# Softmax weights of the first 24 steps normalised by the product that turns them

## The chip, the core and the metric

The kernel runs on one core of a Trainium2 chip. The metric is the device time of one execution in microseconds (us). The engines are PE (TensorE), DVE (VectorE), ACT (ScalarE), POOL (GpSimd) and SP (SyncE, which only starts transfers). Each of them takes its instructions in the order in which they stand.

## What is computed

A windowed attention for 4 batches of 8 heads, 768 positions and 64 channels. Each query sees the first 8 keys and the 96 keys up to its own, with a bias that grows with the distance. Behind it stands a gated projection over 512 channels.

```python
scores = scale * (q @ k.T) + bias                  # 0.125, -slope[h] * distance
scores = where(keep, scores, -1e9)                 # keep: key < 8, or 0 <= query - key < 96
a = exp(scores - max(scores))
a = a / (sum(a) + 1e-9)
x = a @ v                                          # heads side by side: 512 channels
gate = sigmoid(sum_k conv_w[k] * shifted(x, k))    # 5 taps along the sequence
out = (gate * (x @ w_val)) @ w_out
```

## The kernel before

**Groups and steps.** The attention is cut into 32 groups g of one batch, one half of the sequence (384 queries) and one pair of heads. Four groups in a row make a phase: one batch and half, all 8 heads; there are 8 phases. A group has three steps s of 128 queries, 96 in all. A step holds its scores for the two heads j in 168 columns each (96 + 8 + 64); the very first step of each sequence has 128.

**The kinds of operation**, by the names that the tables use:

- S g (L624): PE multiplies queries and keys of a group into two PSUM banks, one for each head, as products of 64 rows by 64 columns.
- AM s,j (L632): DVE adds the bias, scales, and keeps the row's minimum. S of the next group waits for the AM of this one.
- EX s,j (L643): ACT takes the exponential into the tile `p` and adds up each row's sum in `sm`.
- RG, RC (L650, L654): the sums of a batch of steps are guarded and inverted into `rs`. The first three steps are batches by themselves, after that a batch has three steps in a first half and two in a second half of the sequence.
- NM s,j (L660, L662): `p` is multiplied row by row with the reciprocal sum, on POOL, DVE or ACT.
- PT (L675): PE turns `p` of a whole batch, 64 query rows at a time, into the two banks `pt`. It is a transposition by the identity, with 104 or 128 columns of `p` loaded as weights and 64 columns streamed: four of them for a step of 128 columns and six for any other.
- EV (L297, L299): ACT or DVE copies the two banks into `ab`, and PT of the next batch waits for that.
- PV (L702, L709): PE multiplies values and turned weights of two groups into `x`.
- XS, XH, XL, CV, SG: `x` is copied out, split into a high and a low part for PE, and filtered by five taps into `gate`.
- VM (L836): PE multiplies phase, output block m and input block c, three products of 384 columns each. GM, GH, GL (L843 on) gate the result and split it.
- OM, OE, ST (L859, L871): PE projects to the output in products of 512 columns; the result is copied out and stored.
- W..., WS (L539 to L541): the weights come as 64-bit numbers and are taken apart; WS is PE's part of that, for the first four blocks.
- WARM and F (L406): products of constants into a bank that nobody reads. WARM stands at the program's start; the three F have 4, 7 and 6 products.

**What sets the order.** Nothing is scheduled at run time. `SLOTS` is a table with a place for every operation, `ENGINES` a table with the engine of those that may run on more than one; the program is written out in the order of the places. `plan.ring` adds the waits of a set of buffers: with `P_B = 7` tiles `p`, for example, EX of a step waits for the PT that frees the tile used seven steps ahead.

Of the kernel before, what the change touches and what calls it, by code (L numbers as in the profile page):

```python
# [16 lines left out]
WARM, FILL_N = 10, (4, 7, 6)  # L17
# [3 lines left out]
HEAD_STEPS, RS_B = 3, 3  # L21
W_PARTS = (2, 2, 2, 2, 2, 1, 1, 1)
# [3 lines left out]
        1, 4, 6, 17, 93, 122, 124, 168, 173, 251, 294, 298, 353, 405, 437, 444, 604, 608, 615, 619, 650, 705, 822,  # L26
        917, 921, 983, 1008, 1012, 1060, 1221, 1227, 1358,
    ),
    "LB": (3,),
    "LV": (  # L30
        18, 97, 129, 134, 177, 182, 209, 213, 240, 247, 349, 409, 428, 432, 497, 501, 710, 713, 724, 727, 813, 816,
        914, 991, 1002, 1064, 1211, 1215, 1224, 1353, 1356, 1496,
    ),
    "WARM": (2,),
    "F": (22, 86, 50),
    "IOTA": (0,),
    "UNITS": (15,),
    "CNT": (7,),
    "DIST": (9, 13),
    "BIAS": (16, 21, 12, 24, 39, 20, 11, 19),  # L40
# [10 lines left out]
    "CWL": (10,),  # L51
    "CWA": (113,),
    "CW": (117,),
    "S": (
        14, 37, 67, 106, 142, 180, 217, 254, 311, 347, 394, 434, 473, 504, 535, 591, 642, 696, 726, 787, 817, 894,
        919, 978, 1041, 1087, 1117, 1170, 1220, 1292, 1363, 1447,
    ),
# [1115 lines left out]
```

## Time and profile before

| | us |
|---|---|
| median of 3 runs | 258.26 (257.35 to 259.97) |
| the profiled execution | 257.78 |
| its span, first to last instruction | 255.7 |
| PE busy | 246.2 (96%) |
| DVE busy | 225.1 (88%) |
| ACT busy | 188.5 (74%) |
| POOL busy | 141.0 (55%) |

The profile is of one execution, and its time is 2.1 us over its span. Shares of busy time are means over stages with different limits, and a matmul's record lasts longer than the time until the next one may start, so PE's busy time is read through the distance between starts.

### The profile page before, as it was taken

To read this page: it belongs to the slowest core of one execution; us is meant where nothing else is said; L and a number is where in the kernel's file an instruction comes from. 1 tells how busy PE (TensorE), PEld (TensorE's weight loads), DVE (VectorE), ACT (ScalarE), POOL (GpSimd) and SP (SyncE) were. 2 spreads that over 40 slices of the span, in tenths; PEclk is the share of its full clock that TensorE was granted. 3 is DMA by queue.
4 is the path that set the end of the run, shared out by engine and by line. 5 is a ranking of instruction groups with operands and counts; after the bars stand their busy time and mean duration, and the time that the engine had idled before them with its cause. 6 is when DMAs were issued, how large, how long until landed. Compare 5 with 4: busy or idle time off the path is not lost.

```text
span 255.7 us, 8994 instructions
## 1 busy us (share of the span) xinstructions
PE 246.2 (96%) x3384; PEld 207.5 (81%) x3386; DVE 225.1 (88%) x783; ACT 188.5 (74%) x643; POOL 141.0 (55%) x240
## 2 busy tenths in 40 slices
PE   8878899999999999999999999999999999999993
PEld 3546678887879987898888998899889889888983
DVE  4999999999999999999999899988999896169940
ACT  3899999999989998888795999685457545055410
POOL 5697999999786687426435554435405602631210
PEclk9999999999999999999999999999999999999998
DMA  5859996367315661532337600650160041010203
GB/s 152 319 179 326 380 359 222 126 219 255 124 45 171 240 235 45 163 119 66 134 122 266 208 3 4 207 225 3 56 224 0 3 154 73 0 44 3 82 5 127
DMA packets 16302, 36.36 MB, mean 142 GB/s; under 512 B 1920, under 2 KB 4480, under 8 KB 16256
## 3 DMA queue, kind: packets, MB, share of 16 engines
q1 hardware_dynamic: 16112, 35.75, 40.2%
q8 instruction: 28, 0.46, 0.7%
q14 instruction: 18, 0.15, 0.2%
q10 hardware_dynamic: 144, 0.00, 0.0%
HBM read 29.46 MB, written 6.29 MB: 140 GB/s over the span
## 4 chain that ended last, share of the span: by engine, by line
PE 50%; DVE 33%; ACT 6%; POOL 6%; issue 3%; DVEq 0%; POOLq 0%
PE o L859 17%; PE val L836 16%; DVE gate L794 11%; DVE t L632 8%; PE s L624 5%; PE pt L675 4%; POOL p L662 4%; PE x L709 3%; ACT p L643 3%; DVE p L662 2%; PE warm L406 2%; PE x L702 2%; DVE g L843 2%; DVE ab L299 2%; DVE xl L786 1%
## 5 line engine op out<-in xcount | busy, mean ns | idle before, releaser
L643 ACT ACTIVATE p<-t,mins 128x168 f32<-128x168 f32 (+1 forms) x192 | 81.0, 427 | 10.3 <-PE pt L675 4.8
L794 DVE SCALAR_TENSOR_TENSOR gate<-xs,cwt,gate 128x384 f32<-128x384 f32 x128 | 81.8, 657 | 1.2 <-ACT gate L796 0.4
L662 POOL TENSOR_SCALAR p<-p,rs 128x168 f32<-128x168 f32 (+1 forms) x100 | 54.9, 559 | 18.3 <-DVE rs L654 13.2
L632 DVE CUSTOM_DVE_ANT_0 t<-s,bias 128x168 f32<-128x168 f32 (+1 forms) x192 | 53.8, 316 | 2.4 <-PE s L624 2.4
L836 PE MATMUL val<-xh,wvh 128*128 128x384 f32 x128 | 44.8, 350 | 0.1
L836 PE MATMUL val<-xl,wvh 128*128 128x384 f32 x128 | 43.3, 338 | 0.1
L836 PE MATMUL val<-xh,wvl 128*128 128x384 f32 x128 | 43.2, 338 | 0.0
L859 PE MATMUL o<-woh,gh 128*128 128x512 f32 (+1 forms) x100 | 39.9, 399 | 0.0
L859 PE MATMUL o<-wol,gh 128*128 128x512 f32 (+1 forms) x100 | 38.6, 386 | 0.0
L859 PE MATMUL o<-woh,gl 128*128 128x512 f32 (+1 forms) x100 | 38.6, 386 | 0.0
L624 PE MATMUL s<-kq 64*64 64x64 f32 (+3 forms) x1088 | 36.6, 264 | 1.7 <-DVE mins L632 0.9
L650 POOL TENSOR_SCALAR sm<-sm 128x4 f32<-128x4 f32 (+2 forms) x32 | 11.0, 344 | 49.1 <-ACT p L643 47.3
L624 PEld LDWEIGHTS s<-kq 64*64 64x64 f32 x1088 | 31.4, 133 | 8.2 <-issue 4.2
L643 ACT ACTIVATION_READ_ACCUMULATOR p<-t,mins 128x1 f32 x192 | 37.3, 194 | 0.0
L297 ACT COPY ab<-pt 128x384 f32<-128x384 f32 (+3 forms) x60 | 29.1, 494 | 9.6 <-PE pt L675 9.3
L850 POOL TENSOR_TENSOR gl<-g,gh 128x384 fp32r<-128x384 f32 x21 | 23.1, 1104 | 19.7 <-ACT gh L297 7.6
L675 PEld LDWEIGHTS pt<-ident,p 64*104 64x104 f32 (+1 forms) x544 | 19.2, 131 | 10.2 <-issue 5.1
L675 PE MATMUL pt<-ident,p 64*104 64x64 f32 (+1 forms) x544 | 25.0, 226 | 1.2 <-DVE cw_h L596 1.1
L836 PEld LDWEIGHTS val<-xh,wvh 128*128 128x128 f32 x128 | 24.0, 188 | 2.2 <-DVE ob L873 0.4
L660 ACT ACTIVATE p<-p,rs 128x168 f32<-128x168 f32 (+1 forms) x55 | 22.5, 426 | 4.2 <-DVE rs L654 4.2
L836 PEld LDWEIGHTS val<-xl,wvh 128*128 128x128 f32 x128 | 24.1, 188 | 0.9 <-DVE xl L786 0.5
L709 PE MATMUL x<-ab,va 104*64 104x128 f32 (+1 forms) x384 | 24.7, 277 | 0.0
(157 smaller groups left out, 414.4 us busy)
## 6 DMA issues: line engine op xcount, KB each, us to landing
kq<-in_kq SPq DMA_DIRECT2D x16, 444.0 KB, 5.7
va<-in_va SPq DMA_DIRECT2D x16, 384.0 KB, 4.3
out<-ob SPq DMA_DIRECT2D x24, 256.0 KB, 2.6
kq<-in_kq SPq DMA_DIRECT2D x15, 392.0 KB, 5.5
va<-in_va SPq DMA_DIRECT2D x16, 320.0 KB, 4.8
w<-in_wv SPq DMA_DIRECT2D x8, 256.0 KB, 5.4
w<-in_wo SPq DMA_DIRECT2D x3, 512.0 KB, 3.5
w<-in_wo SPq DMA_DIRECT2D x2, 256.0 KB, 5.6
```

What stands on the lines that cost most here:

```text
L297: nc.scalar.copy(dst, src)
L624: nc.tensor.matmul(s[rows, u : u + w], T["rq", g][r, k * P + half * QH : k * P + (half + 1) * QH], T["rk", g][r, c : c + w], start=True, s ...
L632: nc.vector.tensor_tensor_reduce(out=t[:, :n], in0=T["s", s // HB, s % HB, j][:, :n], in1=bias[:, h, :P] if n == P else bias[:, h, P:], op ...
L643: nc.scalar.activation(T["p", s][:, j, :n], T["t", s, j][:, :n], AF.Exp, bias=mins[:, s, j : j + 1], scale=-1.0, accum_out=T["sm", batch_o ...
L660: nc.scalar.mul(pr, pr, rs)
L662: engine(e).tensor_scalar(out=pr, in0=pr, scalar1=rs, scalar2=1.0, op0=ALU.mult, op1=ALU.mult)
L675: nc.tensor.transpose(pts[h][:m, c0 : c0 + QH], pr[rows, c : c + m], ident[rows, rows])
L709: nc.tensor.matmul(T["x", g][rows(i), c0 : c0 + P], T["near", g][:n, k, j], T["a", HB * g + k][:n, j * P : (j + 1) * P], start=False, stop ...
L794: nc.vector.scalar_tensor_tensor(out=gt, in0=src, scalar=w, in1=gt, op0=ALU.mult, op1=ALU.add)
L836: nc.tensor.matmul(T["val", ph, m], (wvh, wvh, wvl)[r][:, m, c * P : (c + 1) * P], (T["xh", g], T["xl", g], T["xh", g])[r], start=(c == 0 ...
L850: engine(e).tensor_sub(tile_of(("gl", ph, m), [P, HT], F32R, "gl", 5), T["g", ph, m], T["gh", ph, m])
L859: nc.tensor.matmul(T[key][:, cols], (T["gh", ph, c], T["gl", ph, c], T["gh", ph, c])[r][:, rows], (woh, woh, wol)[r][:, c, cols], start=(c ...
```

## The change

In the first 24 steps (12 batches) there is no NM. Instead a new operation DG on DVE or POOL builds, for each batch, one 64 by 64 diagonal of reciprocal sums for every step and head and each half of the rows, in one instruction: the identity folded to 128 rows of 64 columns (FOLD, once) times `rs`. PT then multiplies `p` with this diagonal where it multiplied with the identity. These are products, not transpositions, and each block of 104 or 128 columns is cut in two, since its columns belong to two heads or must land at partition 0 and at 64. There is one buffer for the diagonals (`DG_B = 1`), so a DG waits for the PT of the batch ahead. F keeps its first four products; thirteen are gone. Places and engines of all operations are new.

```diff
-WARM, FILL_N = 10, (4, 7, 6)
+WARM, FILL_N = 10, (4,)
+DIAG_STEPS, DG_B = 24, 1
...
-        "VVGVGGGGGGGSVGGSGSGVSGGSGGGGGGGSGGGVGSGGGGVGGGGSSGSGSGSGGVSGGGGVSGGGGGGGVSSVGVGGVSGGSGSSGVVGGGSG"
+        "SGSGGGGGGSVSSSGSGGSGSGSSGSSGVSVSVGGSSGSGSSGSVSGSSSSVSGSSSGSVGSSGGGVGGSVSVSGGVVGSVGGGSSSGGSSSVGGG"
...
+    "DG": (41, 51, 95, 102, 135, 164, 195, 239, 258, 278, 307, 321),
...
+    "DG": "GVVGVVVVGVVG",
...
+    def fold_ident(e):
+        T["fold",] = const.tile([P, QH], F32, name="fold")
+        engine(e).tensor_add(T["fold",], ident[:, :QH], ident[:, QH:])
...
+    def diag(e, ss):
+
+        n = 2 * len(ss)
+        t = tile_of(("dg", ss[0]), [P, 2 * HB, QH], F32, "dg", DG_B)
+        engine(e).tensor_tensor(out=t[:, :n], in0=T["fold",].unsqueeze(1).to_broadcast([P, n, QH]),
+                                in1=T["rs", ss[0]][:, :n].unsqueeze(2).to_broadcast([P, n, QH]), op=ALU.mult)
+
+    def turn(ss):
+
+        c0 = 0
+        for s in ss:
+            pr = T["p", s].rearrange("p two n -> p (two n)")
+            n = width(s)
+            m = P if n == P else SH
+            near = [[(c, 0, QH, j), (c + QH, QH, m - QH, j)] for j, c in ((0, 0), (1, SW if n == P else 2 * SW - SH))]
+            for block in near + ([] if n == P else [[(SH, 0, QH, 0), (SW, QH, QH, 1)]]):
+                for h in range(2):
+                    rows = slice(h * QH, (h + 1) * QH)
+                    for c, r, w, j in block:
+                        nc.tensor.matmul(pts[h][r : r + w, c0 : c0 + QH], pr[rows, c : c + w],
+                                         T["dg", ss[0]][rows, 2 * (s - ss[0]) + j], start=True, stop=True)
                 c0 += QH
...
-                         [("RG", ss[0])] + plan.ring("rs", RS_B, key, [("NM", t, j) for t in ss for j in range(2)]))
-            for j in range(2):
+                         [("RG", ss[0])] + plan.ring("rs", RS_B, key, [("DG", ss[0])] if ss[0] < DIAG_STEPS else
+                                                     [("NM", t, j) for t in ss for j in range(2)]))
+            folded = ss[0] < DIAG_STEPS
+            if folded and s == ss[-1]:
+                key = ("DG", ss[0])
+                plan.add(key, (DVE, POOL), lambda e, ss=ss: diag(e, ss),
+                         [("RC", ss[0]), ("FOLD",)] + plan.ring("dg", DG_B, key, [("PT", ss[0])]))
+            for j in () if folded else range(2):
                 plan.add(("NM", s, j), (POOL, DVE, ACT), lambda e, s=s, j=j: norm(e, s, j), [("RC", batch_of[s])])
...
-                plan.add(key, (PE,), lambda e, ss=ss: transpose(ss),
-                         [("NM", t, j) for t in ss for j in range(2)] + [("IOTA",)] + bank)
+                plan.add(key, (PE,), lambda e, ss=ss, turned=turn if folded else transpose: turned(ss),
+                         ([("DG", ss[0])] if folded else [("NM", t, j) for t in ss for j in range(2)] + [("IOTA",)])
+                         + bank)
```

What this moves is seen at three places. On PE, the first two PT stood around the second F (`p_184` and `p_195` are the weights of steps 0 and 1, the `s` that follows is group 2's):

```order
L675 MATMUL pt_89<-ident,p_184 128x64
L675 MATMUL pt_90<-ident,p_184 128x64
...
L406 LDWEIGHTS const-bfloat16-1.0
L406 MATMUL warm<-const-bfloat16-1.0 128x512
...
L675 MATMUL pt_89<-ident,p_195 104x64
L675 MATMUL pt_90<-ident,p_195 104x64
...
L675 MATMUL pt_89<-ident,p_195 128x64
L675 MATMUL pt_90<-ident,p_195 128x64
L624 MATMUL s_0_283<-kq_131 64x128
```

and now follow each other as products of 64 by 64 and 40 by 64:

```order
L706 MATMUL pt_89<-dg_229,p_187 64x64 x2
L706 MATMUL pt_90<-dg_229,p_187 64x64 x2
...
L706 MATMUL pt_89<-dg_254,p_198 64x64
L706 MATMUL pt_89<-dg_254,p_198 40x64
L706 MATMUL pt_90<-dg_254,p_198 64x64
L706 MATMUL pt_90<-dg_254,p_198 40x64
...
L706 MATMUL pt_89<-dg_254,p_198 64x64 x2
L706 MATMUL pt_90<-dg_254,p_198 64x64 x2
L633 MATMUL s_0_289<-kq_135 64x128
```

The F between them is gone, and every product of PT has the 64 by 64 shape of the S that follows. On POOL, the batch of steps 3 to 5 (`rs_340`) had five of its six NM behind each other:

```order
L650 TENSOR_SCALAR sm_256<-sm_256 128x6
L662 TENSOR_SCALAR p_228<-p_228,rs_306 128x168
L498 TENSOR_SCALAR ('w', 1)_z<-w_135 128x512
L662 TENSOR_SCALAR p_270<-p_270,rs_340 128x168
L662 TENSOR_SCALAR p_280<-p_280,rs_340 128x168
L662 TENSOR_SCALAR p_255<-p_255,rs_340 128x128
L662 TENSOR_SCALAR p_270<-p_270,rs_340 128x168
L662 TENSOR_SCALAR p_255<-p_255,rs_340 128x128
L650 TENSOR_SCALAR sm_321<-sm_321 128x6
```

and has one DG in their place (`rs_392`):

```order
L507 TENSOR_SCALAR ('w', 1)_z<-w_139 128x512
L502 TENSOR_SCALAR ('w', 1)_y<-w_139 128x512
L659 TENSOR_SCALAR sm_252<-sm_252 128x6
L691 TENSOR_TENSOR dg_398<-fold,rs_392 128x384
L659 TENSOR_SCALAR sm_330<-sm_330 128x6
L507 TENSOR_SCALAR ('w', 2)_z<-w_322 128x512
```

What filled POOL between two guards is one instruction now, and preparation of the weights moves up. On PE again, from the S of group 6 (`s_0_688`, now `s_0_739`) to that of group 7 (`s_0_807`, now `s_0_870`) there stood PV, PT, the first VM (`val_0`), and only behind S the WS of weight block 3:

```order
L624 MATMUL s_0_688<-kq_440 64x168
...
L702 MATMUL x_718<-ab_614,va_450 64x64 x2
...
L675 MATMUL pt_89<-ident,p_548 104x64
...
L836 MATMUL val_0_792<-xh_625,wvh 128x384
...
L624 MATMUL s_0_807<-kq_573 64x168
...
L539 MATMUL pt_90<-('w', 3)_h,ident 128x512
```

and now the first VM and one more (`val_1`) stand ahead of both S, and that WS between them:

```order
L875 MATMUL val_0_697<-xh_635,wvh 128x384
...
L875 MATMUL val_1_711<-xh_635,wvh 128x384
...
L633 MATMUL s_0_739<-kq_459 64x168
...
L706 MATMUL pt_89<-dg_732,p_548 64x64
...
L734 MATMUL x_799<-ab_609,va_607 64x64 x2
...
L548 MATMUL pt_90<-('w', 3)_h,ident 128x512
...
L633 MATMUL s_0_870<-kq_637 64x168
```

So PE has one WS and one VM more behind it when it comes to group 7's S.

## Rows read from the trace of the kernel before

**Rows 1.** The page: span, busy time and instructions, and slices of 6.4 us

```profile
span 255.7 us, 8994 instructions
PE 246.2 (96%) x3384; PEld 207.5 (81%) x3386; DVE 225.1 (88%) x783; ACT 188.5 (74%) x643; POOL 141.0 (55%) x240
...
DVE  4999999999999999999999899988999896169940
...
PEclk9999999999999999999999999999999999999998
```

**Rows 2.** Windows of 16 us: busy us of each engine (instructions), clock, DMA

```profile
16.00:32.00 16.00, 13.05 (x292) 9.83 (x294) 15.31 (x65) 15.28 (x59) 13.68 (x24) 1.00 0.98 336
32.00:48.00 16.00, 15.89 (x287) 13.36 (x287) 15.69 (x62) 15.83 (x58) 15.47 (x24) 1.00 0.66 240
...
144.00:160.00 16.00, 16.00 (x315) 14.18 (x311) 14.53 (x57) 15.03 (x53) 9.15 (x17) 1.00 0.05 19
```

**Rows 3.** PE's timeline, 8 to 36 us: start, length, [idle ahead <-releaser]

```profile
8.15 1.31 PE L624 MATMUL s<-kq 64*64 64x128 f32 x32 [0.61 <-DVE mins L632]
...
12.80 1.12 PE L539 MATMUL pt<-('w', 0)_h,ident 128*128 128x512 f32 x2
...
14.27 1.70 PE L406 MATMUL warm<-const-bfloat16-1.0 128*128 128x512 bf16 x6
15.90 0.38 PE L675 MATMUL pt<-ident,p 64*104 64x64 f32 x6
...
18.33 0.69 PE L675 MATMUL pt<-ident,p 64*128 64x64 f32 x16 [1.09 <-DVE cw_h L596]
...
19.70 1.13 PE L539 MATMUL pt<-('w', 1)_h,ident 128*128 128x512 f32 x2 [0.68 <-ACT ab L297]
...
25.86 1.11 PE L624 MATMUL s<-kq 64*64 64x168 f32 x34 [0.30 <-DVE mins L632]
...
28.48 1.12 PE L539 MATMUL pt<-('w', 2)_h,ident 128*128 128x512 f32 x2 [0.62 <-ACT ab L297]
...
34.58 1.11 PE L624 MATMUL s<-kq 64*64 64x168 f32 x36
```

**Rows 4.** POOL's timeline, 13 to 18.4 us

```profile
15.04 3.24 POOL L662 TENSOR_SCALAR p<-p,rs 128x168 f32<-128x168 f32 x5
```

**Rows 5.** The chain that ended last, 140 to 236 us: start, length

```profile
143.39 0.49 PE pt L675 x12
143.88 0.95 PE s L624 x27
144.83 0.70 PE x L702 x47
...
164.16 0.72 PE val L836 x3
...
165.57 0.53 PE val L836 x3
...
172.81 0.62 PE pt L675 x16
...
174.47 0.47 PE x L702 x32
...
229.10 0.84 PE x L702 x24
```

**Rows 6.** Groups by line: busy us, mean ns, idle ahead

```profile
L662 POOL TENSOR_SCALAR p<-p,rs 128x168 f32<-128x168 f32 (+1 forms) x100 | 54.9, 559 | 18.3 <-DVE rs L654 13.2 <-ACT ob L871 3.4 <-PE val L836 0.4
...
L660 ACT ACTIVATE p<-p,rs 128x168 f32<-128x168 f32 (+1 forms) x55 | 22.5, 426 | 4.2 <-DVE rs L654 4.2
...
L786 POOL TENSOR_TENSOR xl<-xs,xh 128x384 fp32r<-128x384 f32 x16 | 17.4, 1089 | 8.7 <-ACT xh L297 8.5
...
L662 DVE TENSOR_SCALAR p<-p,rs 128x168 f32<-128x168 f32 (+1 forms) x37 | 13.5, 374 | 0.1
...
L786 DVE TENSOR_TENSOR xl<-xs,xh 128x384 fp32r<-128x384 f32 x16 | 10.1, 634 | 0.0
```

More of the change, by code (lines that the diff above doesn't have):

```diff
@@ L33 @@
     ),
     "WARM": (2,),
[L35 to L40, printed above, removed]
[10 rows of a table removed]
-    "CWL": (10,),
-    "CWA": (113,),
-    "CW": (117,),
+    "F": (21,),
+    "IOTA": (3,),
+    "UNITS": (18,),
+    "FOLD": (35,),
+    "CNT": (8,),
+    "DIST": (10, 13),
+    "BIAS": (14, 19, 16, 24, 36, 40, 17, 20),
[10 rows of a table added]
+    "CWL": (15,),
+    "CWA": (98,),
+    "CW": (120,),
     "S": (
-        14, 37, 67, 106, 142, 180, 217, 254, 311, 347, 394, 434, 473, 504, 535, 591, 642, 696, 726, 787, 817, 894,
-        919, 978, 1041, 1087, 1117, 1170, 1220, 1292, 1363, 1447,
+        11, 38, 65, 91, 122, 159, 200, 238, 275, 305, 342, 396, 446, 488, 512, 551, 595, 658, 725, 781, 808, 865,
+        892, 949, 1006, 1059, 1124, 1176, 1226, 1266, 1337, 1421,
@@ L105 @@
+        1517,
+    ),
+    "DG": (41, 51, 95, 102, 135, 164, 195, 239, 258, 278, 307, 321),
     "PT": (
[L106 to L108 removed]
+        46, 59, 97, 114, 146, 170, 206, 245, 269, 288, 312, 335, 389, 418, 469, 508, 556, 590, 613, 652, 675, 732,
+        777, 801, 863, 886, 945, 970, 1011, 1057, 1076, 1129, 1173, 1192, 1262, 1334, 1353, 1401, 1419, 1433, 1536,
+        1551,
@@ L109 @@
     ),
     "EV": (
[5 rows of a table removed]
-    ),
-    "WS": (78, 127, 202, 261),
-    "ZH": (35,),
[5 rows of a table added]
+    ),
[10 rows of a table added]
+    ),
+    "ZH": (0,),
     "XS": (
-        171, 188, 253, 249, 387, 374, 476, 469, 570, 578, 643, 670, 781, 731, 846, 860, 942, 926, 1004, 1010, 1125,
-        1129, 1188, 1202, 1310, 1355, 1389, 1397, 1568, 1578, 1591, 1599,
+        147, 150, 228, 262, 340, 386, 436, 421, 490, 542, 637, 619, 704, 712, 802, 834, 897, 924, 1005, 1048, 1102,
+        1081, 1193, 1199, 1287, 1307, 1359, 1414, 1434, 1435, 1559, 1565,
@@ L184 @@
-    "FA": (1577,),
-    "FB": (1650,),
-    "FC": (1652,),
+        630, 564, 618, 720, 731, 965, 946, 962, 1135, 1128, 1131, 1179, 1302, 1318, 1340, 1463, 1469, 1487, 1585,
+        1555, 1583, 1622, 1630, 1637,
+    ),
+    "FA": (1508,),
+    "FB": (1613,),
+    "FC": (1615,),
 }
 ENGINES = {
-    "BIAS": "GGGGGVVS",
+    "FOLD": "V",
+    "BIAS": "GVSGGVSG",
     "BI2": "GV",
-    "WA": "GSGGGSSS",
-    "WZ": "GGGVGGGG",
-    "WH": "SVVGSGGG",
-    "WD": "VGVV",
-    "WP": "GVGVSSSS",
-    "RG": "GGGGGGGGVGGGVGGGVVGGVGGGGGVGGGVGGGGVGGVGVG",
+    "WA": "GGGGGGSS",
@@ L197 @@
+    "WZ": "GGGGGGGG",
+    "WH": "SSSSSGGS",
+    "WD": "GVGV",
+    "WP": "GVVVSSSS",
+    "RG": "GGGGGGGGGGGGGGGVGGGGGGGVVVGGVGGGVGVGGVGVGG",
+    "DG": "GVVGVVVVGVVG",
+    "EV": "SSSSSVSSSSSSSSSSSVSVSSVSSVSVSSSVSSVSSVSVVSSSVSSSVSSSSSSSSVSVSVVSVSSSVSVSSSSSSVSVVSVV",
     "NM": (
-        "VVGVGGGGGGGSVGGSGSGVSGGSGGGGGGGSGGGVGSGGGGVGGGGSSGSGSGSGGVSGGGGVSGGGGGGGVSSVGVGGVSGGSGSSGVVGGGSG"
-        "GGVGSVSVSGGVGGSVGSGSGSVGSGVSVSSVVSSGGVGSGSGGSSGGGSGGGSSSVSGVSGGGSGVVGSVGVVVGSSGSGSGVVSGSGSVSGGSG"
-    ),
@@ L213 @@
+    "HI": "GGSGSVGGGSGGVSSG",
+    "GH": "SSSVSVSSVVVSVSVSSVVSSVSSSVSVSVVS",
+    "GL": "GGVGGGVGGVGGGGVVGVGGVVGGVGGGVGVV",
+    "OE": "SVSVSSSVSSSSSVSSSSVSSSVSS",
 }
@@ L411, in attention_moe @@
     plan.add(("WARM",), (PE,), lambda e: zeros(WARM))
-    for i in range(HB):
+    for i in range(len(FILL_N)):
         plan.add(("F", i), (PE,), lambda e, i=i: zeros(FILL_N[i]), [("S", 0), ("WARM",)])
@@ L436, in attention_moe @@
     plan.add(("UNITS",), (ACT,), signed_units, [("IOTA",)])
+    def fold_ident(e):
+        T["fold",] = const.tile([P, QH], F32, name="fold")
+        engine(e).tensor_add(T["fold",], ident[:, :QH], ident[:, QH:])
+    plan.add(("FOLD",), (POOL, DVE), fold_ident, [("IOTA",)])
     def read_counts(e):
@@ L555, in w_low @@
         engine(e).tensor_add(low, h, T[("w", i), "r"])
-    plan.ring("moe", 2, ("WARM",), [("WARM",)] + [("F", s) for s in range(HB)])
+    plan.ring("moe", 2, ("WARM",), [("WARM",)] + [("F", s) for s in range(len(FILL_N))])
     for i in range(2 * NC):
```

74 lines of the change are left out of this document (32 added, 42 removed), and 137 rows, old and new, of the table SLOTS.

## The prediction

> **What bounds the kernel now.** I read the page first. [...] A busy PE is not yet a bound, so the windows come next: in 16 to 32 us PE does 13.05 us and is the least busy of PE, DVE and ACT; in 32 to 48 us PE, DVE and ACT all stand at 15.7 or more, POOL at 15.47; in 144 to 160 us only PE is at 16.00 [rows 2]. So there are three stages. Up to about 34 us PE waits, and any of three engines may be the reason. From there to about 140 us PE and DVE are both full. After that PE alone sets the end: the chain is made of PE's pieces without a gap between them [rows 5].
>
> PE's timeline shows the waits of the first stage: 0.61 us for AM ahead of S of group 1, 1.09 us ahead of the PT of steps 3 to 5, 0.68 and 0.62 us for EV ahead of two WS, 0.30 us for AM ahead of an S: 3.3 us [rows 3]. The wait of 1.09 us is put down to a small DVE instruction, but POOL's row shows the real cause: five NM of that batch run there from 15.04 to 18.28 us [rows 4]. The changed steps, groups 0 to 7 of 32, lie in the first two stages.
>
> **What goes, what comes, on PE.** All 12 changed batches together have 136 transpositions, which become 272 products (a step of 128 columns: 4 to 8, any other: 6 to 12).
>
> - *A transposition.* A batch of 12 takes 0.49 us in the chain, one of 16 takes 0.62 us [rows 5]: 32.5 ns each, and 0.10 us that a batch costs beside that.
> - *A product.* The nearest row is PV's first part, products with the very same sizes (64 rows, 64 columns, 64 streamed). Each leaves two records. 47 of 48 records for 24 products take 0.70 us, 32 for 16 take 0.47 us [rows 5], 29.2 ns a product with nothing beside it: they run in four quarters of the array at once. The new order of products also goes round the four quarters (two places of `p` rows, two of `pt` rows). So 272 x 29.2 = 7.9 us against 136 x 32.5 = 4.4 us: +3.5 us.
> - *The change of shape.* The 0.10 us of a batch is what PE loses as it goes from one tile shape to another; VM shows the same, three products take 0.72 us behind S-like work and PT, 0.53 us behind OM, which has VM's shape [rows 5]. That is 0.10 to 0.19 us a time. PT now has the shape of S and of PV's first part. In the listed order of PE I count 126 changes of shape before and 112 after: -14, or -1.4 us at 0.10. With 0.19 instead, a transposition is left with 25 ns: the products then cost +4.5 and the changes of shape give back 2.7, so the sum hardly depends on it: about +2 us. [...]
> - *The fill.* 13 products go. Seven of them took from 14.27 to 15.90 us, 0.233 us each [rows 3], so 3.0 us of PE time. But they stood in a stretch where PE had little else to do; what they held up is the PT behind them and the S of group 3, by 1.63 us at the most.
>
> **What goes, what comes, elsewhere.** 48 NM go: 33 on POOL at 559 ns, 8 on ACT at 426 ns, 7 on DVE at 374 ns [rows 6], 24.5 us of work. 12 DG come, 4 on POOL and 8 on DVE. No row shows one; the nearest is XL, a tensor with a tensor, 384 columns, 1089 ns on POOL and 634 ns on DVE [rows 6]. A DG has 128, 256 or 384 columns, and both operands are read with a repeat. Bounds: a third of XL for the small ones, XL itself for all, so 4 to 9.5 us for the 12; I take 6.5. FOLD is one small instruction. The new places use what POOL gains for weight preparation and for XL, and give ACT more (63 of the later NM instead of 47).
>
> **Where that leaves the first stage.** I compare the two listed orders up to the S of group 7, which starts at 34.58 us [rows 3], just where PE fills up. POOL's list ahead of it has 19 NM less, two DG and some preparation more, about 7 us in all: POOL hardly ends a wait any more. DVE's list has the same 42 AM; twelve instructions leave (5 NM, 2 EV, 4 of weights or XL, 1 guard) and twelve come (5 DG, FOLD, 6 of weights, filter and XS or XH), all of them near the 374 to 634 ns of [rows 6]: the same length within about 1 us. ACT's list too: five NM and some copies less, two EX, three EV and three copies of weights more. So POOL's wait goes and DVE or ACT is late next: S of group 7 still waits for AM, at nearly the time of before. From DVE's idle time in 16 to 32 us, 0.69 us [rows 2], I take that 0.7 us closes: 33.9 us. By that time PE has more behind it: one WS (12.80 to 14.27 us, 1.47 us [rows 3]) and one VM (0.53 us [rows 5]), which before stood behind that S. The longer PT up to there is already paid, in time in which PE waited. Gain at this place: 0.7 + 2.0 = 2.7 us.
>
> **The second stage pays back.** Five of the batches are turned after that, where PE is full: 120 products for 60 transpositions, 3.5 - 1.95 = +1.55 us, and 5 of the 14 changes of shape, -0.5 us: +1.05 us. The DG there wait for RC as the NM did; each also waits for the PT of the batch ahead (one buffer), but in the listed order at least one S or VM stands between that PT and the next, so I cost that at nothing; without that cover, the AM queued behind a DG on DVE would be late, and the next S with them. DVE's whole list is shorter by 12 NM (4.5 us) and longer by 8 DG (2 to 5 us), so it stays as full as PE but no fuller. After 140 us nothing changes for PE.
>
> **Sum.** -2.7 + 1.05 = -1.65 us. The profiled execution took 257.78 us and would take 256.1; against the median of the runs, 258.26, that is 256.6 us.
>
> **Rivals.**
>
> - *More of the waiting goes.* If DVE and ACT, no longer crowded by POOL, run their lists faster, all of PE's 3.3 us of waits and the 3.0 us of fill could be used. The products up to group 7 cost PE about 0.95 us more, so 5.3 us would be gained there instead of 2.7, then 1.05 paid back: -4.25, 254.0 us. For it: POOL's five NM took 0.65 us each in the crowd against a mean of 0.56 [rows 4, 6]. Against it: ACT and DVE are at 15.3 of 16 us already there [rows 2], and their lists don't shrink.
> - *The lead is waited away.* DVE is full until 140 us too. If it sets the pace through the second stage with an unchanged list, PE comes to 140 us when it did, with nothing saved: 258.2 us. DVE's busy 15.69 of 16 beside PE's 15.89 [rows 2] is for it, its shorter whole list against it.
> - *The products run two at a time, not four.* Then the kernel is slower. A PV of one group uses two quarters at once, and its 12 products take 0.84 us, 70 ns each [rows 5]. 272 x 41 ns = 11 us more, of which at least the 120 in the second stage, 4.9 us, lie on the path: 261.5 to 267.7 us. The gain is gone from about 35 ns a product on (1.65 us over 272). The order round the four quarters speaks against it. [...]
> - *The clock falls* in the thinner stretch from 8 to 18 us, without the fill: about 5 us of PE work there at half the clock, +5 us at most, 259 to 262 us. In 16 to 32 us PE waits as much and the rows keep 1.00 [rows 2].
>
> **How the numbers follow.** The forecast 0.45 (255.2 to 257.6 us), more of the waiting gone 0.25 (252.8 to 255.3), the lead waited away 0.18 (257.6 to 259.4), two at a time 0.05, the clock 0.04, something else 0.03. The runs of before spread by 1%, and about 1% is what a measurement can tell. Faster by over 1% is below 255.7 us: the second case and a little of the first, 0.32. Slower is above 260.8 us: 0.11. Within 1%: 0.57. The range from 253.3 to 259.4 us leaves out the lower end of the second case and the two slow mechanisms.
>
> **What the profile after would show.** The products of PT in two records each, 29 ns a product and a batch of 12 in about 0.70 us; if it is 1.5 us, the third rival holds. The PT of steps 3 to 5 no later than 17.5 us and the S of group 4 some two us earlier, but the S of group 7 within a us of 34. POOL below 12 us of 16 from 16 to 48 us, and no wait of PE on it. DVE's DG between 0.2 and 0.65 us. The clock at 1.00 throughout. PE filled from 34 us on. Wrong would be: a wait of DG on PT that moves AM, PE idle for over a us after 40 us, or a stretch at the lower clock.

## The result, and the profile after

The changed kernel takes 262.34 us (median of 6 runs, 260.37 to 262.80) beside 258.72 us for the kernel before, measured with it: 1.013 times as long, 95% interval 1.009 to 1.017. Forecast were 256.6 us, in a range from 253.3 to 259.4 us, so the sign is wrong too. Measured once more (e16) it was 1.010 (1.004 to 1.016). A run over 1.5% longer than the fastest of its kernel counts in the medians but not in the ratios. The profiled execution took 261.67 us, its span is 259.5 us, 3.8 us more than before.

The page after, the lines that answer to [rows 1], and its line on PE's instruction transfers:

```profile
span 259.5 us, 9752 instructions
PE 246.5 (95%) x3781; PEld 209.4 (81%) x3781; DVE 222.4 (86%) x775; ACT 190.9 (74%) x650; POOL 130.1 (50%) x206
...
DVE  3899997999999999999988989988998869868620
...
PEclk9999999999999999999999999999999999999999
...
q8 instruction: 31, 0.51, 0.8%
```

The windows after, as [rows 2]:

```profile
16.00:32.00 16.00, 14.55 (x438) 11.76 (x429) 15.71 (x65) 15.46 (x55) 8.94 (x13) 1.00 0.87 280
32.00:48.00 16.00, 13.28 (x336) 10.79 (x338) 14.23 (x56) 12.11 (x44) 9.72 (x14) 1.00 0.77 289
144.00:160.00 16.00, 16.00 (x223) 13.94 (x223) 14.69 (x44) 12.28 (x41) 11.93 (x17) 1.00 0.16 60
```

PE has 438 records of products in the window from 16 to 32 us where it had 292, as meant, and is busier. But from 32 to 48 us, where PE, DVE and ACT all stood at 15.7 or more, all three now have time to spare: 13.28, 14.23 and 12.11 us. None of the three is full there; something holds all of them up. PE's timeline after, as [rows 3], all places with over 0.15 us ahead from 8 to 54 us and the S of groups 4 and 7:

```profile
8.47 1.31 PE L633 MATMUL s<-kq 64*64 64x128 f32 x31 [0.61 <-issue]
...
10.97 0.67 PE L706 MATMUL pt<-dg,p 64*64 64x64 f32 x22 [0.96 <-ACT ab L300]
...
15.39 1.31 PE L633 MATMUL s<-kq 64*64 64x128 f32 x32 [0.72 <-PE pt L550]
...
18.21 1.16 PE L706 MATMUL pt<-dg,p 64*64 64x64 f32 x64 [1.09 <-POOL dg L691]
19.18 1.24 PE L633 MATMUL s<-kq 64*64 64x168 f32 x36
...
26.88 0.21 PE L633 MATMUL s<-kq 64*64 64x64 f32 x1 [0.28 <-issue]
...
33.24 0.69 PE L706 MATMUL pt<-dg,p 64*40 64x64 f32 x33 [1.23 <-issue]
...
37.30 1.11 PE L633 MATMUL s<-kq 64*64 64x168 f32 x34
39.64 0.27 PE L633 MATMUL s<-kq 64*64 64x64 f32 x2 [1.23 <-issue]
...
45.07 1.29 PE L706 MATMUL pt<-dg,p 64*64 64x64 f32 x48 [0.18 <-DVE dg L691]
...
49.24 0.92 PE L706 MATMUL pt<-dg,p 64*64 64x64 f32 x48 [0.56 <-DVE dg L691]
```

The S of group 4 comes at 19.13 us (by its first weight load), 2.1 us earlier than before, as forecast. The S of group 7 comes at 37.30 us, forecast 33.9. In between, and inside that S itself, PE stands still three times in the middle of an operation (0.28, 1.23 and 1.23 us) with "issue" as the reason: it waited for nothing that the profile shows. I call these pauses. (The 0.61 us at 8.47 us are the wait for AM of [rows 3].) In [rows 3] nothing of the kind is to be seen. POOL's timeline, where [rows 4] had five NM in a row:

```profile
17.25 0.91 POOL L691 TENSOR_TENSOR dg<-fold,rs 128x384 f32<-128x384 f32 x1 [3.07 <-PE pt L706]
```

The chain that ended last after, as [rows 5], 26 to 51 us:

```profile
26.59 0.28 issue
27.09 1.09 PE pt L706 x63
...
32.01 1.23 issue
33.24 0.69 PE pt L706 x31
...
38.41 1.23 issue
39.64 0.27 PE s L633 x2
39.91 0.78 PE pt L706 x46
40.69 1.79 PE val L875 x9
42.48 0.93 PE pt L706 x43
43.48 1.44 DVE dg L691
...
49.24 0.92 PE pt L706 x46
50.16 0.70 PE x L734 x48
```

From 18.2 to 43.5 us the chain is PE's pieces and these three pauses alone: PE is the bound from 18 us on, not from 34. From 43.5 to 49.2 us the chain runs over DVE, from one DG to the next, and then over PE again. The page's shares of the chain by engine, before and after:

```profile
PE 50%; DVE 33%; ACT 6%; POOL 6%; issue 3%; DVEq 0%; POOLq 0%
PE 91%; DVE 3%; issue 2%; ACT 2%; POOL 1%; DVEq 0%; ACTq 0%
```

PE's time by kind, added up from the distances between the starts of its matmuls, with gaps over 0.02 us apart (us, first to last matmul):

```
               before   after
PT              22.65   26.37
S               33.06   31.85
PV              35.86   35.70
VM              70.51   70.05
OM              69.28   69.79
WS               6.04    6.30
WARM and F       8.56    6.12
idle             4.60    8.08   of it: waits to 18.3 us 2.03 / 3.47, 18.3 to 40 us 1.85 / 0.08,
sum            250.57  254.27          40 to 60 us 0.11 / 0.81, later 0.62 / 0.87; pauses 0 / 2.85
```

The work grew by 0.2 us. Nearly all of the loss is idle time, +3.5 us, and 2.85 of that are the pauses (the three, and a fourth of 0.11 us at 53.05).

**What the pauses are.** I counted PE's records (products, weight loads, waits for semaphores) in order of their starts and set them beside the packets of the instruction queue, 16,384 bytes each; the page counts 28 of them before and 31 after. The rows are a choice. "Pause" is the distance between the starts of the two records around it, "behind" the time from the packet's end to the record at which PE goes on (us). The distance is up to 0.3 us longer than the idle time that the timelines show:

```
kernel                record   pause   packet           goes on   behind
changed                  961    0.50    24.48 to  25.48    26.88     1.40
changed                 1217    1.45    30.84 to  31.83    33.24     1.42
changed                 1473    1.45    37.02 to  38.10    39.64     1.55
52 records more (e3)    1217    1.83    30.07 to  31.03    32.44     1.41
no fill (e6)             961    1.59    35.12 to  36.01    37.36     1.35
112 records more (e11)   705    1.95    19.14 to  20.07    21.59     1.52
112 records more (e11)  1473    2.38    37.01 to  38.06    39.52     1.45
dense stretch (e10)     9153    2.12   280.13 to 281.08   282.44     1.36
dense stretch (e10)     9409    1.85   283.88 to 284.82   286.17     1.35
```

All record numbers are 193 plus a multiple of 256, in every kernel. I read this so: PE's instructions come in blocks of 256, and PE stands still at a block's limit where the next block isn't there yet. In all 18 traces packets and limits go one to one, 511 limits in all, and PE never passes a limit sooner than 1.11 us behind its packet's end; at the 50 limits with more than 0.3 us between the records around them it is 1.21 to 1.59 us. In the kernel before, its records passed each limit 1.78 us or more behind the packet, so it never stood still there. In the timelines a late block cost PE up to 2.1 us in these kernels, and 3.4 us at the first limit within e10's dense stretch.

An fp32 product of PT leaves four records, two passes of a weight load and a product each (after: 544 and 544 for the 272), a transposition two (before: 544 and 544 for 544). So a batch of 12 transpositions was 24 records and its 24 products are 96, and S (72 records), PT (96 to 128) and PV's first part (64 or 96) now stand behind each other as one dense run.

### The profile page after: what moved, and what is told of

Its sections match the earlier page's. It is cut to its first block, busy times and chain, and to the rows that moved or that the text cites. A ratio compares the mean times of both kernels' runs of the same rounds, so it can differ in the third digit from the quotient of the medians.

```text
span 259.5 us, 9752 instructions
## 1 busy us (share of the span) xinstructions
PE 246.5 (95%) x3781; PEld 209.4 (81%) x3781; DVE 222.4 (86%) x775; ACT 190.9 (74%) x650; POOL 130.1 (50%) x206
## 4 chain that ended last, share of the span: by engine, by line
PE 91%; DVE 3%; issue 2%; ACT 2%; POOL 1%; DVEq 0%; ACTq 0%
PE o L898 27%; PE val L875 26%; PE s L633 11%; PE x L741 9%; PE pt L684 6%; PE x L734 4%; PE pt L706 3%; PE warm L409 2%; ACT p L652 1%; PE pt L548 1%; DVE dg L691 1%; DVE t L641 1%; PE pt L549 0%; POOL dg L691 0%; PE pt L409 0%
## 5 line engine op out<-in xcount | busy, mean ns | idle before, releaser
L671 POOL TENSOR_SCALAR p<-p,rs 128x168 f32<-128x168 f32 (+1 forms) x56 | 34.2, 618 | 19.0 <-DVE rs L663 13.4
L875 PE MATMUL val<-xl,wvh 128*128 128x384 f32 x128 | 43.2, 338 | 0.0
L633 PE MATMUL s<-kq 64*64 64x64 f32 (+3 forms) x1088 | 35.9, 264 | 2.9 <-issue 2.1
L300 ACT COPY ab<-pt 128x384 f32<-128x384 f32 (+3 forms) x59 | 28.5, 496 | 8.3 <-PE pt L684 5.1
L825 POOL TENSOR_TENSOR xl<-xs,xh 128x384 fp32r<-128x384 f32 x19 | 20.5, 1081 | 14.5 <-DVE xh L302 11.3
L669 ACT ACTIVATE p<-p,rs 128x168 f32<-128x168 f32 (+1 forms) x63 | 25.2, 424 | 3.2 <-DVE rs L663 3.0
L910 ACT ACTIVATE ob<-o 128x512 f32<-128x512 f32 (+1 forms) x19 | 10.8, 574 | 22.2 <-PE o L898 22.1
```

The lines of the kernel that those rows point to most:

```text
L300: nc.scalar.copy(dst, src)
L633: nc.tensor.matmul(s[rows, u : u + w], T["rq", g][r, k * P + half * QH : k * P + (half + 1) * QH], T["rk", g][r, c : c + w], start=True, s ...
L669: nc.scalar.mul(pr, pr, rs)
L671: engine(e).tensor_scalar(out=pr, in0=pr, scalar1=rs, scalar2=1.0, op0=ALU.mult, op1=ALU.mult)
L825: engine(e).tensor_sub(tile_of(("xl", g), [P, HT], F32R, "xl", XH_B), xs[g % XS_B][:, HIST:], T["xh", g])
L875: nc.tensor.matmul(T["val", ph, m], (wvh, wvh, wvl)[r][:, m, c * P : (c + 1) * P], (T["xh", g], T["xl", g], T["xh", g])[r], start=(c == 0 ...
```

## Experiments

Ratios are to the kernel before, measured with each, with their intervals. A profile is of one execution; those of e3, e5, e12 and e13 are the fastest of their kernel, 1.4 to 2.4 us below its median. "Theories": *instruction blocks* (above); *one buffer* (DG waits for the PT ahead); *slow products*; *the new order*.

**e1, two buffers for the diagonals.**

```diff
+        if list(batches).index(ss[0]) % 2:
+            t = tile_of(("dg", ss[0]), [P, 2 * HB, QH], F32, "dg", 1)
+        else:
+            t = T["dg", ss[0]] = xs[4][:, HIST:].rearrange("p (n q) -> p n q", q=QH)
```

> The changed kernel with two buffers for the diagonals (every other batch builds its diagonal in a tile that is free until the XS of group 4), nothing else moved. Theory 'one buffer': DG's waits for the PT of the batch ahead go (three on POOL of 5.8 us in all, one of 0.53 us on DVE), PE's waits for DG of 1.09 and 0.56 us go with them, and the S of group 7 comes about 1 us earlier than 37.3 us: 1 to 2.5 us faster than the changed kernel. Theory 'instruction blocks' (PE stood still at 26.4, 31.8 and 38.2 us for 0.5, 1.45 and 1.45 us, each time at a record that is 256 after the last, and 1.4 to 1.55 us after a packet of the instruction queue): these holes stay, and the time moves by less than 1 us. Theory 'slow products': no change, within 0.5 us.

Measured: 261.75 us, 1.011 (1.006 to 1.016). The S of group 7 at 37.38 us, pauses of 0.39, 1.43, 0.93 and 0.24 us. POOL's DG of steps 3 to 5:

```profile
16.58 1.17 POOL L694 TENSOR_TENSOR dg<-fold,rs 128x384 f32<-128x384 f32 x1 [2.82 <-DVE rs L663]
```

The buffer's wait is gone, and the DG waits for RC nearly as long (2.82 us instead of 3.07) and takes longer (1.17 us instead of 0.91); PE's 1.09 us ahead of that PT stayed. The buffer was not what held it: the wait named was the last of two that ended almost together.

**e2, another order of the products.**

```diff
-                for h in range(2):
-                    for c, r, w, j in block:
+                for h, (c, r, w, j) in ((0, block[0]), (1, block[1]), (0, block[1]), (1, block[0])):
```

> The changed kernel, the four products of a pair of pieces in the order (rows 0, columns 0), (rows 64, columns 64), (rows 0, columns 64), (rows 64, columns 0), so that two products in a row never share a half of the array's rows or columns. Theory 'slow products' (24 products took 0.78 to 0.93 us where 0.70 was assumed, since two in a row stand on the same rows): a batch of 24 products takes 0.70 us, 272 products save 2 us of PE time, and 1 us or more of it shows in the time, since PE is full from 40 us on. The other two theories: the batch takes less or not, but the holes and the waits for DG stay, and the time moves by less than 0.7 us.

Measured: 262.05 us, 1.012 (1.006 to 1.017). In the chain the batches of 24 products still take 0.78, 0.93 and 0.93 us. The order within the four quarters made no difference.

**e3, e4 and e11, the changed kernel with 52, 152 and 112 records more in WARM.**

```diff
-WARM, FILL_N = 10, (4,)
+SMALL = 29                       # e4: 5 and 81, e11: 6 and 60
+WARM, FILL_N = 7, (4,)
...
+        for _ in range(SMALL if first else 0):
+            nc.tensor.matmul(T["warm",][:16, :16], nc.const_aps.tensor(1.0, [P, 16], BF16),
+                             nc.const_aps.tensor(1.0, [P, 16], BF16), start=True, stop=True)
```

> The changed kernel with 26 products more in WARM (7 of 512 columns and 29 of 16 columns for 10 of 512), so that every later instruction of PE stands 52 records further on and the block limits fall 52 records earlier in the program. Theory 'instruction blocks': from the starts of the records in the changed kernel, the limits up to 60 us then fall behind stretches of 100 records that take 4.3, 2.9, 1.4, 3.5, 3.5, 2.1, 2.9, 2.0 and 4.8 us, where they were 2.4, 2.5, 1.8, 1.2, 3.2, 1.0, 1.8, 1.7 and 1.4; a hole opens where such a stretch is well under 2.4 us. The two holes of 1.45 us go and one of up to 1 us is left near 21 us; the S of group 7 comes at about 35.5 us, and the time falls by 1.5 to 3 us. The other two theories: no change, within 0.5 us.

> As the kernel with 52 records more, but with 152 more (5 products of 512 columns and 81 of 16 in WARM). Theory 'instruction blocks': the limits fall in the dense stretches, by the same reckoning about twice as much is lacking up to 120 us as in the changed kernel (14 us against 7.5 us, not all of it in the path): holes at other places and more of them, and a time 1 to 4 us longer than the changed kernel's. The other two theories: no change, within 0.5 us, apart from what a later end of WARM may cost (up to 1 us if S of group 0 comes that much later).

> The changed kernel with 112 more records in WARM (6 products of 512 columns and 60 of 16 for 10 of 512). Theory 'instruction blocks': by the record numbers of the changed kernel the limits then fall at 849 (PT behind PV, 23.9 us), 1105 (VM and WS, 29 us), 1361 (PV's second part, 34.5 us), 1617, 1873 and 2129; the two holes of 1.23 us go, what opens instead is under 0.8 us each, so the idle time of PE falls by 1 to 2.5 us and the S of group 7 comes at 34.5 to 36 us; 1 to 2 us faster than the changed kernel. Other theories: no change, within 0.5 us.

Measured: e3 261.35 us, 1.010 (1.006 to 1.013); e4 267.22 us (261.6 to 269.3), with a ratio of 1.018 (1.008 to 1.027) that rests on two runs and settles little; e11 265.73 us, 1.024 (1.017 to 1.030). e3 was to be 1.5 to 3 us faster than the changed kernel and is 1 us below its median. In e3 the pause at 39.6 us went and that at 26.9 us shrank to 0.14, but one of 1.53 us stood at 32.44 us, in the S of group 6, and one of 0.42 at 49.98. e11 came out the opposite way: five pauses, 6.3 us in all, the worst in PV and in S. PE's waits in it (us in total, times, longest; the second row holds the 0.60 us ahead of the S of group 1 too):

```profile
PE x L747 <- issue: 3.2, 2, 2.1
PE s L639 <- issue: 3.2, 3, 1.7
```

So the place of the limits is worth some 4 us between e3 and e11, with the same work and order behind WARM. Part of e11's loss is a granted clock of 0.985 in the profiled run: it is at 0.50 from 22.7 to 26.1 and from 39.8 to 43.2 us, right behind the pauses of 1.73 and 2.11 us. But its two runs at 1.00 took 264.5 and 265.5 us. Where a limit hurts I could not reckon from the starts of the changed kernel: up to 60 us a packet began 69 to 199 records ahead of its limit there, 32 to 183 in e3 and 5 to 221 in e11, and I found no rule for that.

**e5, the diagonals in the order of before.** `SLOTS`, `ENGINES` and the fill of before; each DG in the place of its batch's first NM, with two buffers as in e1.

> The diagonals alone: order, engines and fill of the kernel before, the 48 NM of the first 24 steps taken out and each DG put where the first NM of its batch stood (two buffers, on the engines of the changed kernel), so the 816 more records of PE are there but not the new order. Theory 'instruction blocks': PE gets the records of the changed kernel, 3.7 us more of PT work (22.65 to 26.37 us in the two traces) and holes of up to 1.5 us, each at a record 256 or a multiple of it after the last; 259.5 to 263 us. Rival 'the new order' (its lists for DVE, ACT and PE cost what was lost, the diagonals nothing): within 1 us of before, 257.5 to 259.5 us, and no hole without a releaser over 0.5 us.

Measured: 265.87 us, 1.028 (1.023 to 1.033). Slower than either theory had it: PT work is 26.32 us as in the changed kernel, DVE's busy time 230.4 us against 225.1, and the S of group 10 comes at 57.0 us instead of 52.1. The diagonals in the old order cost 7 us; the new order with the fill gone gives some 4 of that back. It has the changed kernel's records but nearly none of its pauses. Those at a limit are 0.45 and 0.21 us, where holes of up to 1.5 us were expected:

```profile
27.28 0.52 PE L443 MATMUL s<-kq 64*64 64x64 f32 x12 [0.45 <-issue]
33.27 0.57 PE L547 MATMUL x<-ab,va 64*64 64x64 f32 x22 [0.21 <-issue]
```

So the records alone don't make the long pauses; the order in which they stand does too. This kernel, with the highest ratio of all, is slow by PE's work, 4.2 us more than before in the profile (PT 3.7 of it), and by other waits: PE's idle time is 6.1 us instead of 4.6.

**e6, the kernel before without 13 products of the fill.**

```diff
-WARM, FILL_N = 10, (4, 7, 6)
+WARM, FILL_N = 10, (4,)
...
-    "F": (22, 86, 50),
+    "F": (22,),
```

> The kernel before with the 13 products of the fill left out, nothing else. From the rows: F took 1.63 us ahead of the PT of step 1 and 1.25 us ahead of that of step 0; if PE only waits longer for AM and NM instead, no change; if all of it is in the path, 2.9 us faster. Both theories on the changed kernel let it be 0 to 1.6 us faster; the granted clock stays at the upper level. By 'instruction blocks' the block limits fall 26 records later, which by the reckoning from starts changes the lack by less than 0.3 us.

Measured: 260.02 us, 1.004 (1.001 to 1.007): not faster but a little slower. What F covered are waits, for EV (1.04 and 0.87 us on PE now) and for a copy of weights (0.77 us), and the S of group 4 waits 1.29 us for a load of queries and keys. The granted clock is 0.99: for 3.4 us, between the places of the two F that are gone and behind the wait of 1.04 us, it is at its lower level, the 0.50 in the window below. And 26 records fewer put a limit into an S:

```profile
10.60:14.00 3.40, 3.40 (x40) 2.59 (x36) 2.52 (x11) 3.04 (x14) 2.85 (x6) 0.50 0.31 121
...
22.30 1.17 PE L624 MATMUL s<-kq 64*64 64x168 f32 x34 [1.29 <-DMA kq<-in_kq]
...
37.36 0.81 PE L624 MATMUL s<-kq 64*64 64x168 f32 x23 [1.29 <-issue]
```

This kernel has no diagonals. The pause belongs to the place of the limit.

**e7, the kernel before with 152 records more in WARM** (as e4).

> The kernel before with 152 more records in WARM (5 products of 512 columns and 81 of 16 for 10 of 512): its work, its order and its diagonal-free transpositions untouched, only the block limits of PE's instructions moved. Theory 'instruction blocks': limits fall behind denser stretches (lack by the starts of records 3.4 us up to 60 us, 0.85 us as it stands): one to three holes without a releaser, of 0.3 to 1.5 us, at records 256 apart, which the kernel before doesn't have, and 0.5 to 2.5 us slower. Rivals (the holes belong to the products or to the diagonals): no hole, within 0.5 us, or up to 1 us more if WARM ends later.

Measured: 258.71 us, 1.000 (0.997 to 1.003), and no pause at a limit over 0.15 us up to 60 us. My reckoning of where pauses open missed again. With the records of transpositions most places leave room; e6 shows that not all do.

**e8, near blocks as one product each.**

```diff
+                near.append((s, c0, [(c, 0, m, j)]))
...
+        for s, c0, block in near + far:
```

> The changed kernel with the near blocks of 104 or 128 columns turned as one product each (they belong to one head, so one diagonal serves), all of them ahead of the far blocks, which stay cut in two: 176 products for 272, 384 records of PE fewer, but 96 of the products in the shape of the transposition, two at a time. Theory 'instruction blocks': PE's records come 1.5 blocks shorter and the dense stretches thinner, so fewer or shorter holes: 1 to 2.5 us faster than the changed kernel if PT itself takes no longer. Rival (products in the whole shape take 70 ns each, as a PV of one group): 96 x 70 + 80 x 33 = 9.4 us against 272 x 35 = 9.5 us, so no gain in PT, and with one more change of shape for each batch 1 to 2 us slower.

Measured: 261.88 us, 1.015 (1.010 to 1.021). The pauses are gone: PE's idle time is 4.17 us, less than before the change. But PT takes 31.2 us in all, 4.9 more, since a batch that took 0.78 to 0.93 us takes 1.27 to 1.34:

```profile
38.70 1.27 PE pt L711 x32
...
41.74 1.34 PE pt L711 x32
```

The rival held, at a higher price than its 70 ns: with 0.24 us for the 8 cut products, the 8 whole ones of such a batch take (1.27 - 0.24) / 8 = 0.13 us each, changes of shape included; between those they start 0.09 us apart, about three times the 32.5 ns of a transposition of the same shape. Fewer records cure the pauses and cost as much elsewhere.

**e9 and e12, diagonals for the first 6 and 12 steps only.** `DIAG_STEPS = 6` and `12`, NM for the others between the places of DG and PT.

> The changed kernel with diagonals for the first 6 steps only (the four batches turned before 18 us, where PE waits), and NM with transpositions by the identity for steps 6 to 23 (NM spread between the places of DG and PT: per batch of three steps 4 on POOL, 1 on DVE, 1 on ACT; of two steps 2, 1, 1). Theory 'PE is full from 18 us on, and its instruction blocks come late in dense stretches': 208 of the 272 products go, about 2.8 us of PT work and 624 records with them; the holes of 1.2 us go too: 257 to 258.5 us, 3.5 to 5 us faster than the changed kernel. Rival 'DVE, ACT and POOL set the pace there': 36 NM come back (20 of them 0.56 us on POOL, 8 or 9 each of 0.4 us on DVE and ACT), PT waits for them, 260 to 263 us.

> As the kernel with six steps, with diagonals for the first 12 steps (six batches, the first 28 us) and NM for steps 12 to 23. 'PE is full from 18 us on': between the six-step kernel and the changed kernel, about 128 products as 64 transpositions, 1.7 us of PT work more than with six: 258.5 to 260.5 us. Rival 'DVE, ACT and POOL set the pace': no slower than the six-step kernel, or faster.

Measured: 1.017 (1.011 to 1.024) and 1.012 (1.007 to 1.017), 264.1 and 262.9 us where the kernel before had 260.5. Six steps come out behind twelve by the medians, though the intervals overlap; 257 to 258.5 us were forecast for them. Pauses are fewer (1.23 us in e9, 0.61 in e12), but PE waits for the NM instead; e9:

```profile
PE pt L494 <- POOL p L481: 1.5, 2, 0.9
...
PE val L685 <- DVE xl L635: 0.9, 1, 0.9
```

The rival held. At these places in the new order NM has no room, and products and NM cost about the same.

**e10, a long dense stretch by itself.**

```diff
+        for _ in range(96):
+            for r, c in ((0, 0), (1, 1), (0, 1), (1, 0)):
+                rows = slice(r * QH, (r + 1) * QH)
+                nc.tensor.matmul(pts[r][c * QH : (c + 1) * QH, :QH], one32[rows], one32[rows], start=True, stop=True)
```

> The kernel before with 384 products of 64 by 64 by 64, constants by constants, round the four quarters, behind WARM and 384 more behind the last PT; nothing waits within them. It measures how PE runs a long dense stretch. Theory 'instruction blocks': inside a block 29 ns a product, as PV's first part; at every 256th record, 64 products, a pause of 0.5 to 1.5 us, so 64 products take 2.4 to 3.4 us instead of 1.9, at the start, where transfers are many, and at the end, where there are almost none. Rival (a product costs 37 ns or the pauses come from waits that the profile doesn't show): 29 to 37 ns throughout, no pauses, 11 to 14 us for 384.

Measured (one run): PE's timeline of the second stretch. It stands at 248.5 us of the kernel before, where the DMA share is 0.16 (246 to 251 us):

```profile
278.44 2.10 PE L408 MATMUL pt<-const-float32-1.0 64*64 64x64 f32 x128 [1.59 <-issue]
282.44 2.10 PE L408 MATMUL pt<-const-float32-1.0 64*64 64x64 f32 x128 [1.91 <-issue]
286.17 2.10 PE L408 MATMUL pt<-const-float32-1.0 64*64 64x64 f32 x128 [1.63 <-issue]
289.90 1.96 PE L408 MATMUL pt<-const-float32-1.0 64*64 64x64 f32 x116 [1.63 <-issue]
```

Each row is one block: 64 products, 128 of the records of products and as many weight loads. Within a block a product takes 29.7 ns, but the blocks start 4.00, 3.73 and 3.73 us apart: 58 to 62 ns a product. In the first stretch they are 3.45 to 4.00 us apart from 12.3 us on (DMA share of the kernel before, 4.5 to 27 us: 0.82). So the supply, not the array, sets the pace of this long dense run.

**e13 and e15, VM moved into the pauses; e16, the changed kernel beside e15.** e13 puts the two VM that stood ahead of the S of group 6 behind it, and one from behind the S of group 7 ahead of it; e15 leaves one of the first two and takes two of the others.

```diff
-        179, 253, 282, 294, 185, 257, 263, 299,
+        200.3, 237.5, 282, 294, 200.6, 257, 263, 299,     # e13
+        179, 237.5, 282, 294, 200.6, 237.7, 263, 299,     # e15
```

> The changed kernel with three VM moved on PE and nothing else: the two that stood ahead of the S of group 6 go between that S and its PT, and one that stood behind the S of group 7 goes ahead of it. So the dense stretches in which PE stood still for 1.23 us each get 1.1 and 0.5 us of VM in front of the block limit, while the block is fetched; work, records and products are the same. Theory 'instruction blocks': the two holes shrink from 2.5 to about 1 us together, 1 to 1.5 us faster than the changed kernel, and the time given back stays to the end, since PE is full from there. Rival (the waits for AM, DG and EV set the pace and PE's holes only stand in front of them): no change, within 0.5 us, or slower where S of group 7 comes later.

> The changed kernel with three VM moved on PE: one of the two ahead of the S of group 6 stays (it covers the EV that the WS behind it waits for, a wait of 0.65 us that opened when both were moved), the other goes between that S and its PT, and two that stood behind the S of group 7 go ahead of it. Theory 'instruction blocks': the wait of 0.65 us closes to about 0.1, about 0.6 us of the pause at the first place comes back, the pause of 0.6 us in the S of group 7 nearly goes; 1.5 to 2.5 us faster than the changed kernel of the same call. Rival (what two VM gained was the chip's): within 0.7 us of the changed kernel.

> The changed kernel itself, to stand beside the one with VM moved: 1.013 times the kernel before if the chip makes no difference, with the pauses at the same records (961, 1217 and 1473) and of 0.3 to 1.5 us.

Measured: e13 260.35 us, 1.008 (1.005 to 1.012); later e15 260.77 us, 1.006 (1.002 to 1.009), beside e16 with 262.47 us, 1.010 (1.004 to 1.016). e13, at the two places:

```profile
32.06 0.93 PE L543 MATMUL pt<-dg,p 64*64 64x64 f32 x48
...
38.56 0.33 PE L470 MATMUL s<-kq 64*64 64x104 f32 x4 [0.59 <-issue]
```

The first pause is gone, the second halved, and a wait of 0.65 us for EV opened at 28.3 us; from the S of group 0 to that of group 16 it takes 76.24 us (5.34 to 81.58), 78.48 in the changed kernel's profile (5.86 to 84.34), and what is gained stays to the end. e16 has its pauses at records 961, 1217 and 1473 again (0.20, 1.12 and 0.93 us), besides 0.17 and 0.39 at 705 and 2241; e15 keeps 0.91, 0.21 and 0.17 us. With the same records and work, filling pauses brought 1.7 us by the medians of e15 and e16, 1.2 us by their ratios. Both kernels stay behind the kernel before.

**e14, products of one pass.**

```diff
-        t = tile_of(("dg", ss[0]), [P, 2 * HB, QH], F32, "dg", DG_B)
+        t = tile_of(("dg", ss[0]), [P, 2 * HB, QH], BF16, "dg", DG_B)
...
+                T["p", s] = short[:, : 2 * SW].rearrange("p (two n) -> p two n", two=2)
```

> The changed kernel with the exponentials and the diagonals of the first 24 steps rounded to the 16-bit type, so that each product takes one pass, two records of PE instead of four (544 fewer in all), in the same shapes and quarters; the weights of these steps are less exact. Theory 'instruction blocks': the dense stretches hold 48 to 64 records of PT instead of 96 to 128, holes nearly go (under 0.6 us in all up to 60 us), and with PT no dearer than the transpositions were (22 to 23 us over the run) the forecast's gain is left: 256 to 258.5 us. Rival (order and waits cost it): PT gets cheaper by 3 us, but PE waits instead, 260 to 262 us.

Measured: 263.05 us, 1.017 (1.012 to 1.021). PT falls to 21.4 us and no pause stands at a block limit (one of 1.10 us without a releaser lies elsewhere), yet PE's idle time is 9.6 us: it waits for DVE's RC (1.52 and 0.69 us) and for DG (1.42 us).

```profile
PE s L633 <- DVE rs L666: 2.2, 2, 1.5
PE pt L709 <- POOL dg L694: 1.4, 1, 1.4
```

The granted clock falls to 0.984: it is at 0.50 from 20.4 to 23.8 us, behind the wait for DG, and from 44.3 to 47.7 us, behind the 1.10 us and the 1.52 us. The forecast's gain isn't left; the rival held. Cheaper products don't help while the chain EX, RC, DG is late.

## Why the prediction was wrong

- **The step that failed** is the first stage's gain: "S of group 7 still waits for AM, at nearly the time of before", closing to 33.9 us with PE 2.0 us ahead. It was worked out from the lists of DVE and ACT alone, as if PE would still wait there. It came at 37.30 us, 2.7 us later than before instead of 0.7 us earlier; with the 2.0 us ahead that is a loss of 0.7 us at this place where 2.7 us of gain were forecast. PE had become the bound at 18.2 us, since the waits between 18 and 34 us did go (1.85 to 0.08 us), and from there its own list and the pauses at its block limits decide. From the PT of steps 3 to 5 to that S PE works 17.5 us where it worked 14.4 (19.1 us between the two starts less 0.08 of waits and 1.51 of pauses, 16.25 less 1.85). The 3.1 us more are the WS, the VM and the longer PT, which the prediction took to fit into time in which PE waited, and the waits there were 1.85 us only. So the list alone brings that S to 35.8 us, an estimate, and the pauses to 37.3. Behind it 1.05 us more were forecast and came out as 3.1 us, 1.23 us of them the pause in that S and 0.74 us waits for DG. I priced products by their time alone, never by how fast PE gets them, though [rows 5] counted the records (47 for 24 products).
- **Part by part, PE's work was sized well.** Products less changes of shape: forecast +2.1 us, measured +1.9 (PT +3.7; S, VM and PV -1.8). Fill: forecast -3.0, measured -2.4. In all -0.9 forecast, +0.2 measured; what OM and WS have more (0.8 us) wasn't in the sum. Left for PE's idle time was -0.75 us; it grew by 3.5 us.
- **The fill** has no term in the sum; the first rival counts its 3.0 us as time to be gained. The waits that it covered came out in its place (0.96 us for EV, 0.72 us ahead of the S of group 3), and e6 shows the kernel before no faster without it.
- **The DG at no cost** was wrong by some 0.7 us: PE waits 0.18 and 0.56 us for DG at 45 and 49 us. The buffer, of which the prediction warned, has a part in them but no price of its own: with two buffers (e1) these waits go, and 0.44 us for XL and 0.25 us for EX come in their place. One DG on DVE took 1.44 us where 0.2 to 0.65 was given.
- **Its list of what the profile would show:** S of group 4 two us earlier, POOL below 12 us of 16, the clock at 1.00: right. PT of steps 3 to 5 by 17.5 us: 18.21, behind DG on POOL, so PE does wait for POOL, 1.09 us as before: the five NM were not all that held it up. A batch of 24 products in 0.70 us: 0.78 to 0.93.
- **The rivals.** *Products two at a time* gave 261.5 to 267.7 us, and the time lies there, but not by that mechanism: e10 has 29.7 ns within a block. What it gave as a price, 70 ns, is near the 58 to 62 ns that e10's long dense run costs through its supply. In e8 whole products take about three times as long as transpositions of the same shape (0.09 us against 32.5 ns); those in four quarters don't (0.78 to 0.93 us for 24, 33 to 39 ns each). *The lead is waited away* had the place (between 34 and 60 us) but DVE as the cause; DVE has 14.23 of 16 us there, though the chain does run over it from 43.5 to 49.2 us. *More of the waiting goes* is out: the waits from 18 to 34 us went, but those ahead of them grew by 1.4 us and the pauses came. *The clock falls* is out for the changed kernel's profile, which keeps 1.00. At the place that this rival named, the clock did fall, to 0.50, in e6, which leaves out the same fill, and in e3, the changed kernel with another WARM (10.4 to 13.8 us); it fell elsewhere in e11 and e14.

How much of the loss the pauses make isn't settled to the us: they are 2.85 us of the profiled span, of which filling them in e15 got back 1.2 to 1.7 us beside e16. Three kernels with few pauses or none (e5, e8, e14) are no faster than the changed kernel, since in each PE's work or its other waits grew. The rest of the 3.6 us are, in the profile, the early waits, DG, and 0.25 us more waiting at the end. What starts a fetch stays open.

## What to carry to other kernels

Count the records that a change adds to an engine, not only their time: at four records for a product of 29 ns, PE ran out of instructions here where PT, S and PV stood together at a block limit. Between two dense operations put one with long instructions (here two VM, 1.2 us in 12 records), and after every edit look again at where pauses without a releaser stand, since a few records more or less move them. When a wait on one engine is to go, add up the lists of all engines ahead of the place, that of the engine that waits among them.

## What the runs showed of the hardware that was not expected

- In all 18 traces PE's instructions come in blocks of 256 records, by packets of 16,384 bytes that take 0.9 to 2.1 us; where PE had to wait for one, it went on 1.2 to 1.6 us behind the packet's end. The long dense run of e10 got a block every 3.45 to 4.0 us, in both of its stretches.
- In e8 an fp32 product with 64 rows by 104 or 128 columns of weights cost about 0.13 us (0.09 us without the changes of shape) where its two pieces, in four quarters, cost 0.06 to 0.08 in the changed kernel.
- Shifting a kernel by 60 records of WARM (e3 to e11), with nothing else changed, moved its time from 1.010 to 1.024 times the kernel before. Behind two of e11's pauses PE ran 3.4 us each at a granted clock of 0.50.
